# Attention and two MoE layers on one Trainium2 core: two jobs change between VectorE and ScalarE, and two query tiles share one PSUM evacuation

## The chip, the cores and the metric

The kernel runs on one core of a Trainium2 chip. The metric is device time in microseconds from the start of the program to its end; three runs of the kernel before gave 1155.38, 1155.15 and 1152.6 us, median 1155.15 us. All engine names are those of the profile: PE is TensorE, DVE is VectorE, ACT is ScalarE, POOL is GpSimd, SP is the queue that issues the DMAs.

## The reference

Thresholded softmax attention over 4 sequences of 576 tokens with 8 heads of 64, then two feed-forward layers over the 2304 tokens (512 to 2048 to 512 columns each):

```python
scores = scale * np.matmul(q, k.transpose(0, 1, 3, 2))
thresh = np.max(scores, axis=-1, keepdims=True) - tau
scores = np.where(scores >= thresh, scores, -1000000000.0)
attn = softmax(scores)                     # over the last axis
x = (attn @ v), heads side by side         # (2304, 512)
h = x @ moe_w_in;  x = (h * np.clip(h + 3.0, 0.0, 6.0) / 6.0) @ moe_w_out
h = x @ moe2_w_in; out = (np.maximum(h, 0.0) ** 2) @ moe2_w_out
```

The weights arrive as 64-bit floats. The kernel needs them as 32-bit floats and then as two parts of reduced precision (a high and a low part) for TensorE.

## The kernel before, in words

The work falls into attention (4 sequences, 4 pairs of heads each, 9 query tiles of 128 rows per pair: 144 score tiles) and eight feed-forward blocks (layer 1 and layer 2 for each sequence). The attention of sequence 0 runs first and alone; the attention of sequence b+1 is interleaved with the two feed-forward blocks of sequence b. In the last 250 us only feed-forward is left.

**One score tile.** PE multiplies q by k into a PSUM tile `s` (L244 for sequence 0, L248 later). DVE reduces it to the row minimum `nm` (L254; the scores are negated, so this is the maximum). The threshold `thr` is `nm` plus the constant `tau_a` (L255: on POOL for sequence 0, on DVE for the three later sequences). ACT makes the exponential `e` with `nm` as bias (L261). DVE multiplies it by the comparison with `thr` and sums the row (L268), which is the last read of `s`. ACT and POOL split `e` into two 16-bit parts `p` (L274 to L276), and a DMA transposes them into `pt` (L278).

**The product with v.** `av` (L296) runs five tiles later: 14 matmuls into a PSUM tile `o` from the pool `ps_a` of two buffers. That pool also holds the transposes of q, k and the outputs (`tps`, `xT`) and a small maximum (`vm`, which DVE reads at L202 and works up in L204 to L206). ACT scales each `o` by the reciprocal of the row sum into the SBUF tile `os` (L304, 64 columns per query tile; L301 for the shared tail tile). `finish` transposes `os` for the feed-forward layers.

**The PSUM pool of the matmuls.** `s`, the hidden products `hp` (L525) and the outputs `y` (L559) share the pool `ps_s` of three buffers. A buffer is free again when DVE has read it for the last time: L268 for `s`, L530 or L536 for `hp`, L565 for `y` (ACT, L563, for the first quarter of a block).

**The weights.** 64 chunks of 128 x 512 are loaded as pairs of 32-bit words (`wd`), numbered 0 to 63 in the order of use. `w_convert` makes 32-bit floats of them: ACT scales the high words into `wc` (L462), DVE shifts `wc` left by 3 (L464) and merges the top three bits of the low words into it (L465, result `wraw`), and SP stores the chunk to DRAM for later reuse (L468). Then ACT and POOL split it into `wh` and `wl` (L484, L485). All 64 conversions are over by 393 us; from then on chunks are reloaded from DRAM, and DVE makes `wl`.

A scheduler sets the order on each engine by its own timing model. Once built, every engine runs its instructions strictly in that order.

Of the kernel before, what the change touches and what calls it, by code (L numbers as in the profile page):

```python
# [10 lines left out]
F32 = mybir.dt.float32  # L11
# [3 lines left out]
I32 = mybir.dt.int32  # L15
U16 = mybir.dt.uint16
AF = mybir.ActivationFunctionType
# [5 lines left out]
LAG = 5  # L23
LOADS = (2, 4, 6)
FIRST_W = 14
N_G, N_WC, N_PT = 3, 3, 5
NWD, NRAW = 3, 4
N_S, N_ACC = 3, 2
# [3 lines left out]
def attention_moe_moe_kernel(  # L32
# [191 lines left out]
    def make_jobs(u):  # L224
        js = []
        order = [(0, 0), (0, 1), (0, 2), (0, 3), ("t", 4), (1, 0), (1, 1), (1, 2), (1, 3)]
        for hd, t in order:
            j = Job()
            j.u, j.hd, j.t = u, hd, t
            js.append(j)  # L230
        return js
# [19 lines left out]
    def soft1(j):  # L251
        j.nm = st.tile([P, 1], F32, name="nm")
        j.thr = st.tile([P, 1], F32, name="thr")
        nc.vector.tensor_reduce(out=j.nm, in_=j.s, axis=AX.XY, op=ALU.min)  # L254
        (nc.gpsimd if j.u.b == 0 else nc.vector).tensor_tensor(out=j.thr, in0=j.nm, in1=tau_a, op=ALU.add)  # L255
        if j.u.b == 0:

            j.e = me.tile([P, S], F32R, name="gh", bufs=NQ + 1).bitcast(F32).rearrange("p (a b) -> p a b", a=2)
        else:
            j.e = at.tile([P, 2, HALF], F32, name="e", bufs=2)  # L260
        nc.scalar.activation(out=j.e, in_=j.s, func=AF.Exp, bias=j.nm, scale=-1.0)  # L261
# [21 lines left out]
        nc.gpsimd.tensor_scalar(out=r, in0=r, scalar1=1e-9, scalar2=u.vsc, op0=ALU.add, op1=ALU.mult)  # L283
        nc.vector.reciprocal(out=r, in_=r)

    def av(j):

        u = j.u
        o = ps_a.tile([P, 512], F32, tag="acc", name="o")
        hs = slice(0, 2) if j.hd == "t" else slice(j.hd, j.hd + 1)  # L290
        w = 2 * D if j.hd == "t" else D
        ops = [(i, P, u.v1, i if i <= NT else i - NT - 1) for i in range(2 * NT + 1)]
        ops += [(i, TAIL if i == NT else P, u.v2, i) for i in range(NT + 1)]
        ops.sort(key=lambda x: x[0])
        for i, (c, m, vv, vc) in enumerate(ops):
            nc.tensor.matmul(o[:, 0:w], lhsT=j.pt[0:m, c, :], rhs=vv[0:m, hs, vc, :], start=i == 0, stop=i == len(ops) - 1)  # L296
        if j.n == 0:
            u.os = at.tile([P, NT + 1, P], F32, name="os", bufs=2)
        if j.hd == "t":
            for h in range(2):  # L300
                nc.scalar.activation(out=u.os[own[h], NT, 0:D], in_=o[own[h], h * D:h * D + D], func=AF.Copy, scale=u.sm[own[h], 2 * NT:2 * NT + 1])  # L301
        else:
            c = j.hd * NT + j.t
            nc.scalar.activation(out=u.os[:, j.t, j.hd * D:j.hd * D + D], in_=o[:, 0:D], func=AF.Copy, scale=u.sm[:, c:c + 1])  # L304

    def finish(u, half):

# [21 lines left out]
    def attention():  # L329

        us = []
        for b, p in units:
            u = Unit()
            u.b, u.p = b, p
            us.append(u)
        all_jobs = []
        for i, u in enumerate(us):
            u.i = i
            js = make_jobs(u)
            for n, j in enumerate(js):  # L340
                j.first = n == 0
                j.n = n
                j.last = n == len(js) - 1
            all_jobs += js
        load_qk(us[0], "k")
        setup()
        load_qk(us[0], "q")
        load_v(us[0])
        for _ in prep_steps(us[0]):
            pass  # L350
        load_qk(us[1], "k")
        load_qk(us[1], "q")
        load_v(us[1])
        n = len(all_jobs) // B
        pr = yield from run(us, all_jobs[0:n], None)
        yield from run(us, all_jobs[n:], pr)

    def run(us, all_jobs, pr):
        n = len(all_jobs)
        for i in range(n + LAG):  # L360
# [9 lines left out]
            if i >= 1 and i - 1 < n:  # L370
# [3 lines left out]
                    recips(jj.u, 2 * NT, 1)  # L374
                elif jj.t % 2:
                    recips(jj.u, jj.hd * NT + jj.t - 1, 2)
            done = [i - LAG] if all_jobs[0].u.b == 0 else [i - LAG - 1, i - LAG] if (i - LAG) % 2 else []
            done = [all_jobs[x] for x in done if 0 <= x < n]
            for j in done:
                av(j)  # L380
            for j in done:
                if j.hd == 1 and j.t % 2:
                    finish(j.u, j.t // 2)
            if i < n and pr is not None:
# [68 lines left out]
    def w_convert(i):  # L453


        src, kind, f = wseq[i]
        d = w_raw[i]
        hi = d[:, :, 1]
        c = wt.tile([P, 512], F32, name="wc", bufs=N_WC)
        t = wt.tile([P, 512], F32, name="wraw", bufs=NRAW)  # L460

        nc.scalar.activation(out=c, in_=hi.bitcast(F32), func=AF.Prelu, scale=2.0 ** -112, alpha=2.0 ** 32)  # L462
        ci = c.bitcast(I32)
        nc.vector.tensor_scalar(out=ci, in0=ci, scalar1=3, scalar2=None, op0=ALU.logical_shift_left)  # L464
        nc.vector.scalar_tensor_tensor(out=t.bitcast(I32), in0=d[:, :, 0], scalar=29, in1=ci, op0=ALU.logical_shift_right, op1=ALU.bitwise_or)  # L465
        key = (id(src), kind, f)
        dr = scr.tile([P, 512], F32, name=f"scr{i}")
        nc.sync.dma_start(out=dr, in_=t)  # L468
        wscr[key] = dr
        w_raw[i] = t  # L470
# [205 lines left out]
```

## Time and profile before

| | |
|---|---|
| median of three runs | 1155.15 us |
| the profiled execution's own time | 1153.59 us |
| its span, first to last instruction | 1151.8 us |
| PE busy | 1097.4 us (95%) |
| DVE, ACT, POOL busy | 766.3, 717.2, 592.1 us |
| mean granted TensorE clock over the span | 0.983 |

Busy time is the union of an engine's instructions. The granted clock is a share of full speed: 1.00 is 2.4 GHz and 0.50 is 1.2 GHz, and a value between is a stretch with some of both. The profiled execution's own time is 1.79 us more than its span.

### The profile page before, as it was taken

The numbers are of one execution on the slowest core, as the hardware profiler recorded it, in microseconds if no ns is written. First come the engines' busy times: TensorE is split into PE (matmuls) and PEld (weight loads), VectorE is DVE, ScalarE is ACT, GpSimd is POOL, SyncE is SP. The second block draws the span as 40 slices with busy tenths as digits, with TensorE's granted clock in tenths as the row PEclk, the third lists the DMA queues.
The fourth block names the chain that finished last, engine by engine and source line by source line (L and its number), as shares of the span: only waits on it lengthen the run. The fifth ranks groups of instructions, "written<-read, shape, count | busy, mean of one in ns | idle before, by whom it ended". The sixth has DMA issues, their size and how long they took to land.

```text
span 1151.8 us, 24221 instructions
## 1 busy us (share of the span) xinstructions
PE 1097.4 (95%) x9136; PEld 1041.9 (90%) x9136; DVE 766.3 (67%) x1393; ACT 717.2 (62%) x1345; POOL 592.1 (51%) x654
## 2 busy tenths in 40 slices
PE   6788899988999999999999999999999999999998
PEld 4566798888988999999999999999999999999998
DVE  6887799988788765767766756766756443445342
ACT  7886677767767766656765666666665455434442
POOL 5975577778677654444534355353643242224111
PEclk9998899999999999999999999999999999999999
DMA  8999899889798454566464544544444333223221
GB/s 199 204 177 196 221 249 263 227 242 249 186 263 218 129 141 114 121 135 137 112 141 118 136 124 112 125 116 100 115 120 111 85 107 91 84 83 90 76 65 42
DMA packets 286660, 167.66 MB, mean 146 GB/s; under 512 B 219216, under 2 KB 247888, under 8 KB 286544
## 3 DMA queue, kind: packets, MB, share of 16 engines
q1 hardware_dynamic: 286544, 166.12, 57.7%
q8 instruction: 72, 1.18, 0.4%
q14 instruction: 44, 0.36, 0.1%
HBM read 98.57 MB, written 21.50 MB: 104 GB/s over the span
## 4 chain that ended last, share of the span: by engine, by line
PE 68%; DVE 2%; DMA 2%; issue 1%; ACT 1%; POOL 1%; SPq 0%; DVEq 0%; ACTq 0%
PE y L559 29%; PE hp L525 29%; PE o L296 4%; PE s L248 4%; DMA vraw<-in_v_dram 1%; PE tps L141 1%; DVE wraw L465 1%; PE ot L586 1%; DVE e L268 1%; DMA wd<-in_moe_w_in_dram 0%; PE xT L310 0%; DMA wd<-in_moe_w_out_dram 0%; DVE wc L464 0%; DVE ya L565 0%; DVE nm L254 0%
## 5 line engine op out<-in xcount | busy, mean ns | idle before, releaser
L539 POOL TENSOR_TENSOR gl<-g,gh 128x576 fp32r<-128x576 f32 x128 | 193.2, 1511 | 265.9 <-ACT gh L538 265.1
L559 PE MATMUL y<-gh,who 128*128 128x288 f32 x1024 | 227.4, 303 | 7.1 <-DVE g L530 3.0
L525 PE MATMUL hp<-xh,whi 128*128 128x288 f32 x1024 | 226.4, 303 | 7.8 <-DVE e L268 6.5
L559 PE MATMUL y<-gh,wlo 128*128 128x288 f32 x1024 | 222.3, 298 | 0.0
L525 PE MATMUL hp<-xh,wli 128*128 128x288 f32 x1024 | 221.8, 298 | 0.0
L525 PE MATMUL hp<-xl,whi 128*128 128x288 f32 x1024 | 221.4, 298 | 0.0
L559 PE MATMUL y<-gl,who 128*128 128x288 f32 x1024 | 218.6, 298 | 0.0
L525 PEld LDWEIGHTS hp<-xh,whi 128*128 128x128 f32 x1024 | 164.7, 190 | 10.2 <-issue 3.9
L559 PEld LDWEIGHTS y<-gh,who 128*128 128x128 f32 x1024 | 165.4, 190 | 9.0 <-issue 6.0
L525 PEld LDWEIGHTS hp<-xh,wli 128*128 128x128 f32 x1024 | 166.3, 190 | 0.2
L559 PEld LDWEIGHTS y<-gh,wlo 128*128 128x128 f32 x1024 | 166.2, 190 | 0.1
L525 PEld LDWEIGHTS hp<-xl,whi 128*128 128x128 f32 x1024 | 165.8, 190 | 0.3
L559 PEld LDWEIGHTS y<-gl,who 128*128 128x128 f32 x1024 | 164.5, 190 | 0.0
L296 PE MATMUL o<-v,pt 128*128 128x64 f16 (+1 forms) x2016 | 124.6, 200 | 17.1 <-DMA pt<-gl 8.5
L254 DVE TENSOR_REDUCE nm<-s 128x1 f32<-128x576 f32 x144 | 108.2, 751 | 48.7 <-PE s L248 38.7
L296 PEld LDWEIGHTS <-pt 128*128 128x128 f16 x2016 | 91.9, 99 | 47.8 <-DMA pt<-gl 13.5
L276 POOL TENSOR_TENSOR p<-e,p 128x512 f16<-128x512 f32 x108 | 129.7, 1201 | 0.0
L565 DVE TENSOR_TENSOR ya<-y,ya 128x576 f32<-128x576 f32 (+1 forms) x97 | 71.9, 749 | 79.9 <-PE y L559 79.0
L484 ACT ACTIVATE who<-wraw 128x512 fp32r<-128x512 f32 x128 | 79.6, 628 | 61.9 <-PE y L559 39.4
L268 DVE SCALAR_TENSOR_TENSOR e<-s,thr,e 128x576 f32<-128x576 f32 x108 | 87.9, 814 | 33.0 <-ACT e L261 30.6
L485 DVE TENSOR_TENSOR wlo<-wraw,who 128x512 fp32r<-128x512 f32 x96 | 79.1, 833 | 45.3 <-ACT who L484 42.7
L261 ACT ACTIVATE e<-s,nm 128x576 f32<-128x576 f32 x108 | 79.7, 738 | 34.3 <-DVE nm L254 29.9
(89 smaller groups left out, 1727.0 us busy)
## 6 DMA issues: line engine op xcount, KB each, us to landing
wraw<-scr SPq DMA_DIRECT2D x192, 256.0 KB, 2.7
wd<-in_moe_w_in_dram SPq DMA_DIRECT2D x32, 512.0 KB, 5.3
scr<-wraw SPq DMA_DIRECT2D x64, 256.0 KB, 3.5
wd<-in_moe_w_out_dram SPq DMA_DIRECT2D x32, 512.0 KB, 4.7
kraw<-in_k_dram SPq DMA_DIRECT2D x16, 256.0 KB, 3.4
qraw<-in_q_dram SPq DMA_DIRECT2D x16, 256.0 KB, 3.5
vraw<-in_v_dram SPq DMA_DIRECT2D x16, 256.0 KB, 3.3
out_dram<-wd SPq DMA_DIRECT2D x16, 256.0 KB, 2.9
```

The costliest lines, as they stand in the source:

```text
L248: nc.tensor.matmul(s[:, half, 0:HALF], lhsT=u.qs[sl][:, cs], rhs=u.ks[sl][:, kk, c], start=i == 0, stop=i == len(ops) - 1)
L254: nc.vector.tensor_reduce(out=j.nm, in_=j.s, axis=AX.XY, op=ALU.min)
L261: nc.scalar.activation(out=j.e, in_=j.s, func=AF.Exp, bias=j.nm, scale=-1.0)
L268: nc.vector.scalar_tensor_tensor(out=j.e, in0=j.s, scalar=j.thr, in1=j.e, op0=ALU.is_le, op1=ALU.mult, accum_out=u.sm[:, col:col + 1])
L276: nc.gpsimd.tensor_tensor(out=p16[:, S + TAIL:], in0=e[:, 0:NT * P], in1=p16[:, 0:NT * P], op=ALU.subtract)
L296: nc.tensor.matmul(o[:, 0:w], lhsT=j.pt[0:m, c, :], rhs=vv[0:m, hs, vc, :], start=i == 0, stop=i == len(ops) - 1)
L484: nc.scalar.activation(out=h, in_=t, func=AF.Copy)
L485: (nc.gpsimd if fresh else nc.vector).tensor_tensor(out=l, in0=t, in1=h.bitcast(F32), op=ALU.subtract)
L525: nc.tensor.matmul(hp[:, a, 0:HALF], lhsT=w[:, cs], rhs=x[c][:, a * HALF:(a + 1) * HALF], start=i == 0, stop=i == 3 * NC - 1)
L539: nc.gpsimd.tensor_tensor(out=gl, in0=gf, in1=gh.bitcast(F32), op=ALU.subtract)
L559: nc.tensor.matmul(a[:, k_, 0:HALF], lhsT=w_hl[wuse[(tag, "o", f)]][w][:, cs], rhs=g[f][:, k_ * HALF:(k_ + 1) * HALF], start=i == 0, stop= ...
L565: nc.vector.tensor_tensor(out=y, in0=av_, in1=y, op=ALU.add)
```

## The change

Three things are edited. From chunk 10 on, every second chunk (10, 12, ..., 62: 27 of 64) gets the top bits of its low words from ACT, as a scaled and rounded 16-bit number written over the low words; DVE then does shift and merge in one instruction. The 108 thresholds of sequences 1 to 3 are made by ACT. And for these sequences two query tiles of a head share one PSUM tile `o`, with 28 matmuls one after the other, and one DVE product with the two reciprocals as a broadcast operand writes both into `os`: 48 products in place of 96 ACT instructions. Sequence 0 and the tail tiles keep theirs.

```diff
@@ -23,6 +23,7 @@
 LAG = 5
 LOADS = (2, 4, 6)
 FIRST_W = 14
+FIRST_DVE = 10
 N_G, N_WC, N_PT = 3, 3, 5
 NWD, NRAW = 3, 4
 N_S, N_ACC = 3, 2
@@ -252,7 +253,10 @@
         j.nm = st.tile([P, 1], F32, name="nm")
         j.thr = st.tile([P, 1], F32, name="thr")
         nc.vector.tensor_reduce(out=j.nm, in_=j.s, axis=AX.XY, op=ALU.min)
-        (nc.gpsimd if j.u.b == 0 else nc.vector).tensor_tensor(out=j.thr, in0=j.nm, in1=tau_a, op=ALU.add)
+        if j.u.b == 0:
+            nc.gpsimd.tensor_tensor(out=j.thr, in0=j.nm, in1=tau_a, op=ALU.add)
+        else:
+            nc.scalar.activation(out=j.thr, in_=j.nm, func=AF.Identity, bias=tau_a)
         if j.u.b == 0:
 
             j.e = me.tile([P, S], F32R, name="gh", bufs=NQ + 1).bitcast(F32).rearrange("p (a b) -> p a b", a=2)
@@ -283,25 +287,31 @@
         nc.gpsimd.tensor_scalar(out=r, in0=r, scalar1=1e-9, scalar2=u.vsc, op0=ALU.add, op1=ALU.mult)
         nc.vector.reciprocal(out=r, in_=r)
 
-    def av(j):
-
-        u = j.u
+    def av(js):
+
+        u, j = js[0].u, js[0]
         o = ps_a.tile([P, 512], F32, tag="acc", name="o")
+        if u.os is None:
+            u.os = at.tile([P, NT + 1, P], F32, name="os", bufs=2)
         hs = slice(0, 2) if j.hd == "t" else slice(j.hd, j.hd + 1)
         w = 2 * D if j.hd == "t" else D
         ops = [(i, P, u.v1, i if i <= NT else i - NT - 1) for i in range(2 * NT + 1)]
         ops += [(i, TAIL if i == NT else P, u.v2, i) for i in range(NT + 1)]
         ops.sort(key=lambda x: x[0])
-        for i, (c, m, vv, vc) in enumerate(ops):
-            nc.tensor.matmul(o[:, 0:w], lhsT=j.pt[0:m, c, :], rhs=vv[0:m, hs, vc, :], start=i == 0, stop=i == len(ops) - 1)
-        if j.n == 0:
-            u.os = at.tile([P, NT + 1, P], F32, name="os", bufs=2)
+        for n, j in enumerate(js):
+            for i, (c, m, vv, vc) in enumerate(ops):
+                nc.tensor.matmul(o[:, n * w:n * w + w], lhsT=j.pt[0:m, c, :], rhs=vv[0:m, hs, vc, :], start=i == 0, stop=i == len(ops) - 1)
+        j = js[0]
         if j.hd == "t":
             for h in range(2):
                 nc.scalar.activation(out=u.os[own[h], NT, 0:D], in_=o[own[h], h * D:h * D + D], func=AF.Copy, scale=u.sm[own[h], 2 * NT:2 * NT + 1])
-        else:
+        elif len(js) == 1:
             c = j.hd * NT + j.t
             nc.scalar.activation(out=u.os[:, j.t, j.hd * D:j.hd * D + D], in_=o[:, 0:D], func=AF.Copy, scale=u.sm[:, c:c + 1])
+        else:
+            c = j.hd * NT + j.t
+            r = u.sm[:, c:c + 2].rearrange("p (t o) -> p t o", o=1).to_broadcast([P, 2, D])
+            nc.vector.tensor_tensor(out=u.os[:, j.t:j.t + 2, j.hd * D:j.hd * D + D], in0=o[:, 0:2 * D].rearrange("p (t d) -> p t d", t=2), in1=r, op=ALU.mult)
 
     def finish(u, half):
 
@@ -336,6 +346,7 @@
         all_jobs = []
         for i, u in enumerate(us):
             u.i = i
+            u.os = None
             js = make_jobs(u)
             for n, j in enumerate(js):
                 j.first = n == 0
@@ -374,11 +385,13 @@
                     recips(jj.u, 2 * NT, 1)
                 elif jj.t % 2:
                     recips(jj.u, jj.hd * NT + jj.t - 1, 2)
-            done = [i - LAG] if all_jobs[0].u.b == 0 else [i - LAG - 1, i - LAG] if (i - LAG) % 2 else []
-            done = [all_jobs[x] for x in done if 0 <= x < n]
-            for j in done:
-                av(j)
-            for j in done:
+            x = i - LAG
+            if 0 <= x < n:
+                j = all_jobs[x]
+                if j.hd == "t" or j.u.b == 0:
+                    av([j])
+                elif j.t % 2:
+                    av([all_jobs[x - 1], j])
                 if j.hd == 1 and j.t % 2:
                     finish(j.u, j.t // 2)
             if i < n and pr is not None:
@@ -461,8 +474,14 @@
 
         nc.scalar.activation(out=c, in_=hi.bitcast(F32), func=AF.Prelu, scale=2.0 ** -112, alpha=2.0 ** 32)
         ci = c.bitcast(I32)
-        nc.vector.tensor_scalar(out=ci, in0=ci, scalar1=3, scalar2=None, op0=ALU.logical_shift_left)
-        nc.vector.scalar_tensor_tensor(out=t.bitcast(I32), in0=d[:, :, 0], scalar=29, in1=ci, op0=ALU.logical_shift_right, op1=ALU.bitwise_or)
+        if i < FIRST_DVE or i % 2:
+            nc.vector.tensor_scalar(out=ci, in0=ci, scalar1=3, scalar2=None, op0=ALU.logical_shift_left)
+            nc.vector.scalar_tensor_tensor(out=t.bitcast(I32), in0=d[:, :, 0], scalar=29, in1=ci, op0=ALU.logical_shift_right, op1=ALU.bitwise_or)
+        else:
+
+            d16 = d.rearrange("p f t -> p (f t)").bitcast(U16).rearrange("p (f t) -> p f t", t=4)
+            nc.scalar.activation(out=d[:, :, 0], in_=d16[:, :, 1], func=AF.Copy, scale=2.0 ** -13, bias=-4095.5 / 8192)
+            nc.vector.scalar_tensor_tensor(out=t.bitcast(I32), in0=ci, scalar=3, in1=d[:, :, 0], op0=ALU.logical_shift_left, op1=ALU.bitwise_or)
         key = (id(src), kind, f)
         dr = scr.tile([P, 512], F32, name=f"scr{i}")
         nc.sync.dma_start(out=dr, in_=t)
```

The scheduler sets the order anew. PE has the same order up to the matmul of `vm` that starts at 137.7 us in the profile. Two places show what changes.

DVE, around the reduction `vsc<-vm` of one head pair of sequence 1 (the place at 285 us of the profile; L464 and L465 are shift and merge, L255 the threshold). Before:

```order
L464 TENSOR_SCALAR wc<-wc 128x512
L254 TENSOR_REDUCE nm<-s 128x1
L255 TENSOR_TENSOR thr<-nm,tau_a 128x1
L536 TENSOR_TENSOR g<-g,hp 128x576
L465 SCALAR_TENSOR_TENSOR wraw<-wd,wc 128x512
L464 TENSOR_SCALAR wc<-wc 128x512
L202 TENSOR_REDUCE vsc<-vm 128x1
L465 SCALAR_TENSOR_TENSOR wraw<-wd,wc 128x512
L204 TENSOR_SCALAR vsc<-vsc 128x1
L268 SCALAR_TENSOR_TENSOR e,sm<-s,thr,e 128x576
```

After (L478 and L479 are shift and merge, L484 the merge that shifts, L314 the product of two query tiles, L203 to L207 the work on `vsc`):

```order
L272 SCALAR_TENSOR_TENSOR e,sm<-s,thr,e 128x576
L478 TENSOR_SCALAR wc<-wc 128x512
L484 SCALAR_TENSOR_TENSOR wraw<-wc,wd 128x512
L288 RECIPROCAL sm<-sm 128x1
L203 TENSOR_REDUCE vsc<-vm 128x1
L205 TENSOR_SCALAR vsc<-vsc 128x1
L206 RECIPROCAL vsc<-vsc 128x1
L207 TENSOR_SCALAR vsc<-vsc 128x1
L255 TENSOR_REDUCE nm<-s 128x1
L314 TENSOR_TENSOR os<-o,sm 128x2x64
L555 TENSOR_TENSOR g<-g,hp 128x576
```

The threshold and one of two shifts are gone from this place, a product has come, and the four instructions on `vsc` stand next to each other.

ACT, around the second chunk that the change touches (`p_2101` and `p_2184` are the same two tiles in both; L462 is the scaling of the high words, L304 the evacuation of one query tile). Before:

```order
L274 ACTIVATE p_2101<-e 128x576
L212 ACTIVATE v_2195<-vraw,vsc 128x640
L304 ACTIVATE os<-o,sm 128x64
L261 ACTIVATE e<-s,nm 128x576
L462 ACTIVATE wc<-wd 128x512
L187 ACTIVATE q_st_93<-tps,qs 64x256
L484 ACTIVATE whi<-wraw 128x512
L563 ACTIVATE ya<-y 128x576 x2
L274 ACTIVATE p_2184<-e 128x576
L304 ACTIVATE os<-o,sm 128x64
```

After (L475 is the scaling of the high words, L483 the new instruction on the low words, L259 the threshold):

```order
L278 ACTIVATE p_2101<-e 128x576
L475 ACTIVATE wc<-wd 128x512
L483 ACTIVATE wd<-wd 128x512
L503 ACTIVATE whi<-wraw 128x512
L188 ACTIVATE q_st_93<-tps,qs 64x256
L259 ACTIVATE thr<-nm,tau_a 128x1
L265 ACTIVATE e<-s,nm 128x576
L582 ACTIVATE ya<-y 128x576
L475 ACTIVATE wc<-wd 128x512
L582 ACTIVATE ya<-y 128x576
L188 ACTIVATE q_st_93<-tps,qs 64x64
L278 ACTIVATE p_2184<-e 128x576
```

Each exponential now has its threshold directly ahead of it, the touched chunk has two instructions in a row, and the evacuations L304 are gone from ACT.

## Rows read from the trace of the kernel before

**Rows 1.** Windows, us: engines' busy time (count), PE's granted clock, DMA share, GB/s

```profile
0.00:106.00 106.00, 83.80 (x701) 61.11 (x702) 81.78 (x198) 84.30 (x178) 76.53 (x152) 0.95 0.88 191
106.00:144.00 38.00, 31.10 (x217) 27.67 (x217) 25.99 (x46) 22.94 (x45) 21.94 (x21) 0.82 0.91 222
144.00:400.00 256.00, 237.50 (x1985) 225.22 (x1984) 220.60 (x377) 182.40 (x348) 189.34 (x180) 0.97 0.86 227
400.00:900.00 500.00, 498.01 (x4321) 481.94 (x4320) 336.03 (x636) 322.79 (x603) 238.28 (x259) 1.00 0.51 121
900.00:1152.00 252.00, 247.00 (x1922) 245.97 (x1920) 101.88 (x140) 104.76 (x174) 66.00 (x45) 1.00 0.27 80
```

**Rows 2.** PE's waits from 144 to 400 us: total us, times, longest

```profile
PE hp L525 <- DVE e L268: 5.3, 5, 1.3
PE o L296 <- DVE vsc L202: 3.1, 3, 1.7
PE y L559 <- DVE g L530: 2.7, 1, 2.7
...
PE hp L525 <- ACT g L532: 0.5, 1, 0.5
...
PE hp L525 <- DVE ya L565: 0.3, 1, 0.3
```

**Rows 3.** DVE from 144 to 400 us by line: busy us, mean ns, idle before

```profile
L465 DVE SCALAR_TENSOR_TENSOR wraw<-wd,wc 128x512 int32<-128x512 int32 x53 | 56.0, 1056 | 5.6 <-POOL wlo L485 1.9 <-DMA scr<-wraw 1.4 <-POOL wli L485 1.1
L464 DVE TENSOR_SCALAR wc<-wc 128x512 int32<-128x512 int32 x53 | 42.8, 807 | 11.1 <-ACT wc L462 10.6
...
L255 DVE TENSOR_TENSOR thr<-nm,tau_a 128x1 f32<-128x1 f32 x36 | 18.8, 522 | 0.4
```

**Rows 4.** Three DVE lines over the whole run: duration ns min/median/max

```profile
L255 DVE TENSOR_TENSOR thr<-nm,tau_a x108: 141/159/1426, 106.4 to 893.5; 128x1 f32<-128x1 f32 x108
L464 DVE TENSOR_SCALAR wc<-wc x64: 405/608/1659, 21.1 to 371.3; 128x512 int32<-128x512 int32 x64
L268 DVE SCALAR_TENSOR_TENSOR e<-s,thr,e x108: 797/817/820, 109.7 to 893.7; 128x576 f32<-128x576 f32 x108
```

**Rows 5.** DVE lines over the whole run, for the new product

```profile
L202 DVE TENSOR_REDUCE vsc<-vm 128x1 f32<-128x128 f32 x16 | 4.6, 285 | 5.9 <-PE vm L200 5.8
L318 DVE TENSOR_TENSOR xl<-xT,xh 128x256 fp32r<-128x256 f32 x8 | 3.4, 420 | 4.6 <-ACT xh L317 4.5
```

**Rows 6.** ACT from 144 to 400 us by line

```profile
L462 ACT ACTIVATE wc<-wd 128x512 f32<-128x512 f32 x53 | 35.3, 667 | 14.4 <-DMA wd<-in_moe_w_in_dram 7.8 <-DMA wd<-in_moe_w_out_dram 6.4
L261 ACT ACTIVATE e<-s,nm 128x576 f32<-128x576 f32 x36 | 26.6, 738 | 13.6 <-DVE nm L254 12.9 <-POOL wli L485 0.2
L304 ACT ACTIVATE os<-o,sm 128x64 f32<-128x64 f32 x29 | 8.8, 309 | 6.5 <-PE o L296 6.4
```

**Rows 7.** ACT lines over the whole run, for the threshold

```profile
L301 ACT ACTIVATE os<-o,sm 64x64 f32<-64x64 f32 x32 | 9.8, 307 | 3.8 <-PE o L296 3.5
L320 ACT ACTIVATE xr<-xT 64x64 f32<-64x64 f32 x24 | 5.1, 212 | 0.1
```

**Rows 8.** DVE in order of time before 285 us: start us, us

```profile
278.52 1.29 DVE L464 TENSOR_SCALAR wc<-wc 128x512 int32<-128x512 int32 x1 [0.20 <-ACT wc L462]
...
280.64 0.44 DVE L255 TENSOR_TENSOR thr<-nm,tau_a 128x1 f32<-128x1 f32 x1
...
283.36 1.62 DVE L464 TENSOR_SCALAR wc<-wc 128x512 int32<-128x512 int32 x1
284.90 0.28 DVE L202 TENSOR_REDUCE vsc<-vm 128x1 f32<-128x128 f32 x1
```

**Rows 9.** PE in order of time after it, and the window that follows

```profile
285.23 1.50 PE L296 MATMUL o<-v,pt 128*128 128x64 f16 x28 [1.71 <-DVE vsc L202]
287.64 0.85 PE L525 MATMUL hp<-xh,whi 128*128 128x288 f32 x2 [0.92 <-DVE e L268]
...
288.00:292.00 4.00, 4.00 (x18) 4.00 (x18) 3.91 (x7) 3.12 (x6) 2.81 (x3) 0.50 0.55 164
```

**Rows 10.** DVE and PE in order of time around the longest wait

```profile
247.09 1.91 DVE L465 SCALAR_TENSOR_TENSOR wraw<-wd,wc 128x512 int32<-128x512 int32 x1
...
249.25 0.41 DVE L464 TENSOR_SCALAR wc<-wc 128x512 int32<-128x512 int32 x1
...
252.03 0.72 PE L559 MATMUL y<-gh,who 128*128 128x288 f32 x2 [2.68 <-DVE g L530]
```

**Rows 11.** Windows, the first and second part of the conversions

```profile
144.00:240.00 96.00, 90.93 (x761) 86.64 (x760) 87.24 (x153) 68.91 (x129) 70.55 (x70) 0.98 0.95 249
240.00:400.00 160.00, 146.57 (x1229) 138.58 (x1226) 133.37 (x225) 113.49 (x220) 118.79 (x111) 0.97 0.80 213
```

More of the change, by code (lines that the diff above doesn't have):

```diff
@@ L301, in av @@
                 nc.scalar.activation(out=u.os[own[h], NT, 0:D], in_=o[own[h], h * D:h * D + D], func=AF.Copy, scale=u.sm[own[h], 2 * NT:2 * NT + 1])
+        elif len(js) == 1:
+            c = j.hd * NT + j.t
+            nc.scalar.activation(out=u.os[:, j.t, j.hd * D:j.hd * D + D], in_=o[:, 0:D], func=AF.Copy, scale=u.sm[:, c:c + 1])
         else:
             c = j.hd * NT + j.t
-            nc.scalar.activation(out=u.os[:, j.t, j.hd * D:j.hd * D + D], in_=o[:, 0:D], func=AF.Copy, scale=u.sm[:, c:c + 1])
+            r = u.sm[:, c:c + 2].rearrange("p (t o) -> p t o", o=1).to_broadcast([P, 2, D])
+            nc.vector.tensor_tensor(out=u.os[:, j.t:j.t + 2, j.hd * D:j.hd * D + D], in0=o[:, 0:2 * D].rearrange("p (t d) -> p t d", t=2), in1=r, op=ALU.mult)
     def finish(u, half):
```

## The prediction

> **What bounds the kernel now.** I read the windows first, since one busy share for the whole run mixes three different stages. From 400 us to the end PE has 745.0 of 752 us busy at full clock, of the missing 7 us 5 lie after 900 us [rows 1]. Nothing that other engines do there can give time back, as long as they don't fall behind. Before 106 us the change touches nothing that counts: sequence 0 keeps its threshold on POOL and its evacuations on ACT, and chunks 0 to 9 are converted as before. So the change is won or lost between 106 and 400 us. From 106 to 144 us PE idles 6.9 us at a clock of 0.82, but only four thresholds and chunk 10 are affected there; I count nothing for it. From 144 to 400 us PE is busy 237.5 of 256 us, which leaves 18.5 us idle, and the granted clock of 0.97 is worth another 0.03 x 256 = 7.7 us. That is a pool of 26.2 us [rows 1].
>
> Next, who ends PE's waits in that stretch. Ten of the eleven kinds of wait name DVE, with 20 waits and 18.0 us together; ACT ends one of 0.5 us [rows 2]. PE waits for a PSUM buffer that DVE has yet to read. DVE is busy 220.6 of 256 us (86%), ACT 182.4 (71%) [rows 1]. DVE is the engine that PE waits for, and the conversion of the weights fills it: shift and merge take 42.8 and 56.0 us there, the thresholds another 18.8 us [rows 3].
>
> **What leaves and enters DVE, 144 to 400 us.** The 53 shifts of the stretch are chunks 11 to 63, so 26 of them are touched: 26 x 0.807 = 21.0 us [rows 3]. The 36 thresholds of 0.522 us are 18.8 us [rows 3]. The 29 evacuations that leave ACT [rows 6] come back as about 15 products on DVE. Such a product, 128 elements from PSUM, is not in the trace. Below it lies the reduction of 128 elements from PSUM with 0.285 us, above it the subtraction of 256 elements from PSUM with 0.420 us [rows 5]; the element count speaks for the first, and I take 0.29, 4.4 us in all. The sum is 21.0 + 18.8 - 4.4 = 35.4 us off DVE, which takes it from 220.6 to 185.2 us, from 86% to 72%.
>
> This is the upper end. A threshold lasts 141 ns at best, 159 in the middle and 1426 at worst, a shift 405 to 1659, while the long L268, which reads one operand from PSUM, stays within 797 to 820 [rows 4]. A good part of the two first is thus waiting, and the next instruction of the same kind may take that waiting over. With the shortest durations and the dearest product the relief is 26 x 0.405 + 36 x 0.141 - 15 x 0.420 = 9.3 us. The Trainium skill explains the stretching (SBUF: State Buffer, "SBUF: two separate sides"): a VectorE instruction with two SBUF inputs, or in a two-port mode, and a GpSimd instruction exclude each other for the whole of the instruction. The trace agrees with it in the 159 and 1426 ns, and by that rule the new product, with one operand in PSUM, would not be stretched.
>
> **What enters and leaves ACT there.** The new instruction on the low words has the element count of L462, which reads the high words at the same stride, with 0.667 us [rows 6]: 26 x 0.667 = 17.3 us. That it reads 16-bit words and writes at a stride is not in the trace; the price could be higher, and a rival below uses it. A threshold on ACT has one element and a bias operand. An instruction of 64 columns takes 0.212 us without and 0.307 us with an operand per partition [rows 7]; I take 0.25, so 36 x 0.25 = 9.0 us. By the Trainium skill (ScalarE: Activation LUTs, "What ACT_TABLE_LOAD costs") an activation with such an operand costs about 0.28 us plus its columns; that would make it 10.1 us. The 29 evacuations of 0.309 us that go are 9.0 us [rows 6]. ACT gains 17.3 us, from 182.4 to 199.7 us, 78%. So the two engines change places, but the busier one then stands at 78% and not at 86%.
>
> **What PE gets from it.** I looked at what stood ahead of DVE's late instruction in two waits. At 285.23 us PE had waited 1.71 us for the reduction of `vsc`. DVE had last idled just before 278.52; since then it ran two shifts of 1.29 and 1.62 us and a threshold of 0.44 [rows 8]. One shift and the threshold go, about 1.9 us, and the new order puts the reduction earlier still. This wait goes, and with it the 0.92 us behind it and the four microseconds at half clock that follow [rows 9]. The longest wait, 2.68 us before 252.03, is another matter: a merge of 1.91 us and other work that stays are ahead of it, and only short shifts of the kind of the 0.41 us at 249.25 can go [rows 10]. It mostly stays. I take it that 55% of the 18.0 us goes, 10 us; this share is an estimate between these two examples. Of the 7.7 us lost to the clock about half hang on waits that go: 4 us. Against this I set 3 us for new waits on ACT: each exponential now stands behind its threshold, and each of 26 times two conversions of 0.667 us run before the next evacuation. The sum is 10 + 4 - 3 = 11 us.
>
> From 400 us on DVE has 336.0 of 500 us and ACT 322.8, and PE still idles only 2 us [rows 1]: 72 thresholds leave DVE and 32 products enter it, under the cover of a full PE. I cost that at nothing. If the cover failed, it would be in the two-buffer pool `ps_a`: `o` is now released by DVE's queue, and a late product holds up a transpose. The profiled execution's own time of 1153.59 less 11 is 1142.6. It lies 1.6 us under the median of 1155.15, from which 11 us make 1144.1. I forecast **1143.5 us**.
>
> **Rivals.**
> - *The whole pool goes.* DVE at 72% might no longer hold PE at all: 1154 - 26 = 1128 us. For it speaks that DVE ends 18.0 of 18.5 us; against it the wait at 252, which has other causes. Chance 0.12.
> - *The DMAs set the pace of the conversions.* Their share is 0.95 from 144 to 240 us and 0.80 afterwards [rows 11], and ACT waited 14.2 us for chunks to land [rows 6]. Then the first part gives nothing, and only 240 to 400 us does: 13.4 us idle and 4.8 us of clock, of which a third is 6 us, and some of it comes back as a wait for the next chunk. 1149 us, 2 to 6 us under now. Chance 0.15.
> - *ACT's queue takes the waits over, no change.* The thresholds sit on the way from `nm` to `e` and so of every score tile's release; 36 x 0.25 = 9 us longer there, and 26 pairs of conversions, eat what DVE returns. 1154 us. Chance 0.13.
> - *Slower: the instruction on the low words is dear.* With 182.4 + 9.0 - 9.0 + 26t, ACT reaches the 220.6 us at which DVE holds PE today when t is 1.47 us. From there PE has the same waits at ACT as it had at DVE, and the longer chain of the score tiles, up to 9 us, comes on top: 1155 + 6 = 1161 us. The same end is reached if products on DVE hold up the transposes after 400 us. Nothing in the trace has such a price, but nothing has such an access either. Chance 0.15.
> - *The change does not do what it says.* The order shows the moved instructions where the diff puts them, so I give this none.
>
> **How the numbers follow.** The forecast has 0.45, for 5 to 17 us gained (1138 to 1150). A difference within 0.3%, 3.5 us, is about what a measurement of this kernel can't tell from none. Faster: 0.45 + 0.12 + 0.10 of the DMA rival = 0.67. The same: 0.05 of that rival + 0.13 = 0.18. Slower: 0.15. For 8 times in 10 the range reaches to 1130, most of the way to the whole pool, and on the other side to 1157.5, past the rival without change; what is left out is the slower rival with most of its 0.15 and a little of the first.
>
> **What the changed profile would show.** The shifts must fall to 37, the DVE thresholds be gone, DVE stand near 72% and ACT near 78% until the last conversion. The last conversion should end some 8 to 12 us earlier than 393 us, and everything after it be shifted by as much. PE's idle time before that should be 8 to 11 us, and its waits should name DVE less and ACT more often. The product should last about 0.29 us without stretching, the instruction on the low words under 0.75 us. I am wrong if that one takes over 1.4 us, if PE's waits before 400 us keep their 18 us under other names, or if idle time of more than 3 us appears on PE after the last conversion.

## The result and the profile after

The changed kernel takes 1136.38 us (median of five runs, 1134.32 to 1139.84), the kernel before beside it 1155.15. The ratio is 0.9844, with a 95% interval from 0.9821 to 0.9867: 18 us faster. The forecast was 1143.5 us; the time lies in its range, at 1.6 times the gain. The profiled execution took 1134.32 us with a span of 1132.5 us, 19.3 under the span before. It is the fastest of the five and has their highest granted clock, 0.990 where the five have a median of 0.988.

First the windows of the changed kernel, with the columns of [rows 1] (us, then busy time and count of PE, weight load, DVE, ACT, POOL, then clock, DMA share, GB/s):

```profile
0.00:106.00 106.00, 84.00 (x698) 61.72 (x698) 84.61 (x198) 84.28 (x178) 77.82 (x154) 0.95 0.92 194
106.00:144.00 38.00, 31.79 (x247) 28.93 (x244) 25.46 (x49) 28.28 (x58) 25.43 (x24) 0.87 0.95 235
144.00:400.00 256.00, 244.90 (x2096) 233.60 (x2095) 196.34 (x341) 202.47 (x390) 194.78 (x185) 1.00 0.88 231
400.00:900.00 500.00, 499.68 (x4348) 483.85 (x4347) 316.85 (x590) 316.88 (x599) 228.79 (x250) 1.00 0.52 121
```

From 144 to 400 us PE now idles 11.1 us in place of 18.5, at a clock of 1.00 in place of 0.97. But a fixed window holds more of the program than it did (2096 matmuls where there were 1985), since the program is further along by then: the last merge began at 392.9 us and begins now at 376.0. For loads I therefore compare the stretch from 144 us to the last conversion, here in the kernel before:

```profile
144.00:393.60 249.60, 231.09 (x1930) 219.30 (x1929) 214.83 (x367) 176.94 (x338) 185.39 (x175) 0.97 0.86 228
```

and in the changed one, with what is left up to 900 us:

```profile
144.00:376.70 232.70, 221.92 (x1907) 211.42 (x1906) 182.13 (x313) 185.91 (x360) 177.37 (x170) 1.00 0.92 241
376.70:900.00 523.30, 522.66 (x4536) 506.04 (x4535) 331.06 (x618) 333.44 (x630) 246.20 (x265) 1.00 0.52 121
```

DVE falls from 86% to 78%, ACT rises from 71% to 80%. For the time the clean account is PE's over the whole run, since both kernels issue the same 9136 matmuls. These are the lines of busy time of the pages before and after (busy us, share of the span, instructions):

```profile
PE 1097.4 (95%) x9136; PEld 1041.9 (90%) x9136; DVE 766.3 (67%) x1393; ACT 717.2 (62%) x1345; POOL 592.1 (51%) x654
PE 1088.1 (96%) x9136; PEld 1035.0 (91%) x9136; DVE 718.8 (63%) x1306; ACT 730.4 (64%) x1384; POOL 590.0 (52%) x654
```

PE's busy time falls from 1097.4 to 1088.1 us: 9.3 us for the same matmuls, most of it from the higher mean clock, 0.990 for 0.983 (0.007 x 1152 = 8.1 us). Its idle time falls from 54.4 to 44.4 us, 10.0 us. Together they are the 19.3 us of the span. This split is that of one execution each, and the clock differs between executions of one kernel: the kernel before ran 60 times beside the experiments below, in 1147.4 to 1158.3 us, with clocks from 0.980 to 0.989 and a median of 0.984. By the medians the clock rose by 0.004, which is 4.6 us of 1150, and the rest of the 18 us would be idle time (an estimate from these clocks). By place, the idle time from 144 us to the last conversion went from 18.5 to 10.8 us, that from 106 to 144 us from 6.9 to 6.2; after the last conversion and up to 900 us it was 2.0 and is 0.6.

PE's waits from 144 to 400 us after the change (total us, times, longest; the five longest of ten rows), to be held against [rows 2]:

```profile
PE y L578 <- DVE e L272: 3.2, 5, 1.2
PE hp L544 <- DVE e L272: 3.2, 2, 1.9
PE s L249 <- DVE g L549: 1.5, 1, 1.5
PE tps L142 <- ACT xr L330: 0.9, 1, 0.9
PE hp L544 <- DVE g L549: 0.7, 1, 0.7
```

The wait for `vsc` (3.1 us) is gone and so is the one of 2.68 us. What is left still names DVE, and ACT, with 1.2 us in two waits for 0.5 in one, hardly more than before. At the place of the wait at 285 us, DVE now runs with gaps under 0.1 us from the shift into the reduction:

```profile
266.48 0.95 DVE L478 TENSOR_SCALAR wc<-wc 128x512 int32<-128x512 int32 x1 [0.26 <-ACT wc L475]
267.35 0.68 DVE L484 SCALAR_TENSOR_TENSOR wraw<-wc,wd 128x512 int32<-128x512 int32 x1
268.12 0.16 DVE L288 RECIPROCAL sm<-sm 128x1 f32<-128x1 f32 x1
268.19 0.27 DVE L203 TENSOR_REDUCE vsc<-vm 128x1 f32<-128x128 f32 x1
```

Of the two shifts and the threshold of [rows 8] one shift of 0.95 us is left there; PE starts its `o` at 268.89 us with no wait in front of it, and the granted clock, which stood at 0.50 after that place [rows 9], is 1.00 in every stretch of 4 us from 236 to 300 us.

The prices of the new instructions, over the whole run (duration ns min/median/max, then first to last start):

```profile
L314 DVE TENSOR_TENSOR os<-o,sm x48: 272/283/293, 137.5 to 905.8; 128x128 f32<-128x128 f32 x48
L259 ACT ACTIVATE thr<-nm,tau_a x108: 275/294/312, 107.6 to 872.8; 128x1 f32<-128x1 f32 x108
L483 ACT ACTIVATE wd<-wd x27: 650/669/700, 130.7 to 351.9; 128x512 int32<-128x512 uint16 x27
L484 DVE SCALAR_TENSOR_TENSOR wraw<-wc,wd x27: 664/779/1966, 133.6 to 372.3; 128x512 int32<-128x512 int32 x27
L478 DVE TENSOR_SCALAR wc<-wc x37: 408/730/1593, 20.7 to 356.0; 128x512 int32<-128x512 int32 x37
```

### The profile page after: what moved, and what is told of

The parts are those of the page before. It is cut to its first block, busy times and chain, and to the rows that moved or that the text cites. A ratio compares the mean times of both kernels' runs of the same rounds, so it can differ in the third digit from the quotient of the medians.

```text
span 1132.5 us, 24055 instructions
## 1 busy us (share of the span) xinstructions
PE 1088.1 (96%) x9136; PEld 1035.0 (91%) x9136; DVE 718.8 (63%) x1306; ACT 730.4 (64%) x1384; POOL 590.0 (52%) x654
## 4 chain that ended last, share of the span: by engine, by line
PE 71%; ACT 3%; DVE 2%; DMA 1%; issue 1%; POOL 1%; SPq 0%; DVEq 0%; ACTq 0%; POOLq 0%
PE y L578 30%; PE hp L544 29%; PE o L303 5%; PE s L249 4%; DMA wd<-in_moe_w_out_dram 1%; PE tps L142 1%; PE ot L605 1%; DMA wd<-in_moe_w_in_dram 1%; DVE wraw L484 0%; ACT e L265 0%; PE xT L320 0%; DVE wraw L479 0%; ACT wc L475 0%; ACT wd L483 0%; DVE ya L584 0%
## 5 line engine op out<-in xcount | busy, mean ns | idle before, releaser
L544 PE MATMUL hp<-xh,wli 128*128 128x288 f32 x1024 | 219.0, 295 | 0.0
L544 PE MATMUL hp<-xl,whi 128*128 128x288 f32 x1024 | 218.8, 296 | 0.0
L255 DVE TENSOR_REDUCE nm<-s 128x1 f32<-128x576 f32 x144 | 107.9, 750 | 51.6 <-PE s L249 46.7
L280 POOL TENSOR_TENSOR p<-e,p 128x512 f16<-128x512 f32 x108 | 132.0, 1222 | 0.0
L557 ACT ACTIVATE gh<-g 128x576 fp32r<-128x576 f32 x128 | 86.8, 680 | 13.6 <-DVE g L555 8.0
```

Source lines behind the costliest of these rows:

```text
L280: nc.gpsimd.tensor_tensor(out=p16[:, S + TAIL:], in0=e[:, 0:NT * P], in1=p16[:, 0:NT * P], op=ALU.subtract)
L544: nc.tensor.matmul(hp[:, a, 0:HALF], lhsT=w[:, cs], rhs=x[c][:, a * HALF:(a + 1) * HALF], start=i == 0, stop=i == 3 * NC - 1)
L557: nc.scalar.activation(out=gh, in_=gf, func=AF.Copy)
```

## The experiments

Each ran 5 to 12 times beside the kernel before; ratios are to it, with 95% intervals. Windows, rows and the ends of the conversions are those of one execution of each kernel. My theory was that DVE's load before the last conversion sets the end, so that each edit is worth what it takes off DVE. The rivals: that pairing the outputs gains by itself, and that ACT's load counts as well. To turn ratios into microseconds I multiply their distance from 1 by 1155; the intervals are 1.4 to 3.3 us to either side. One thing holds for all of them: the scheduler sets the order anew for every kernel. Even with the changed kernel as the base, as in d_shift and a_twice, PE's order differs from the change's from 147 or 148 us on. So the price of an edit includes that of its order, and no run separates the two.

| kernel | what of the change it has | ratio | last conversion ends, us |
|---|---|---|---|
| e1_conv | conversion | 0.9932 [0.9908, 0.9955] | 385.2 |
| e2_thr | thresholds | 0.9974 [0.9959, 0.9988] | 396.9 |
| e3_pair | pairs | 0.9930 [0.9909, 0.9950] | 385.9 |
| e4_conv_thr | conversion, thresholds | 0.9917 [0.9892, 0.9943] | 389.1 |
| e5_conv_pair | conversion, pairs | 0.9893 [0.9865, 0.9922] | 382.6 |
| the change | all three | 0.9844 [0.9821, 0.9867] | 376.7 |

**The conversion alone** (e1_conv): the kernel before with this edit only.

```diff
-        nc.vector.tensor_scalar(out=ci, ...shift left 3)
-        nc.vector.scalar_tensor_tensor(... in0=d[:, :, 0], scalar=29, in1=ci, ...)
+        if i < FIRST_DVE or i % 2:
...
+            nc.scalar.activation(out=d[:, :, 0], in_=d16[:, :, 1], func=AF.Copy, ...)
+            nc.vector.scalar_tensor_tensor(... in0=ci, scalar=3, in1=d[:, :, 0], ...)
```

> The kernel before with the split conversion alone (low words of chunks 10, 12, ..., 62 on ACT). Theory (DVE's load until the last conversion sets the time): 26 shifts of 0.81 us leave DVE there, about half of the 35 us that the whole change takes off it, so about half of the 18.8 us: 8 to 11 us faster, the last conversion near 384 us, granted clock 144 to 380 us at 0.98 or above. Rival (the new order of the products with v gives the gain): 0 to 3 us faster.

It gained 7.9 us, just under the theory's 8 to 11. Its window up to the last conversion:

```profile
144.00:385.20 241.20, 225.62 (x1934) 215.43 (x1934) 191.06 (x340) 191.47 (x364) 183.06 (x175) 0.99 0.89 235
```

DVE has 23.8 us less than before and ACT 14.5 more.

**The thresholds alone** (e2_thr).

```diff
-        (nc.gpsimd if j.u.b == 0 else nc.vector).tensor_tensor(out=j.thr, in0=j.nm, in1=tau_a, op=ALU.add)
+        if j.u.b == 0:
+            nc.gpsimd.tensor_tensor(out=j.thr, in0=j.nm, in1=tau_a, op=ALU.add)
+        else:
+            nc.scalar.activation(out=j.thr, in_=j.nm, func=AF.Identity, bias=tau_a)
```

> The kernel before with the thresholds of sequences 1 to 3 on ACT alone. Theory: 18.8 us leave DVE, most of it waiting for GpSimd; the merges may take over some of that waiting: 5 to 9 us faster. Rival (waiting is only handed on, and a threshold costs its 0.14 us): 36 x 0.14 = 5 us of DVE work, 1 to 2 us faster. Second rival (the longer chain through ACT costs): slower by up to 9 us.

3.0 us, the smallest of the three and between the ranges of the theory and its first rival, although 18.8 us of DVE time leave by the rows [rows 3]. The window shows only half of that gone (214.83 to 205.50). Much of the other half is in the merges: their mean rises from 1056 ns [rows 3] to 1184, 6.7 us over 52 of them. First the window, then their row:

```profile
144.00:396.90 252.90, 234.32 (x1987) 222.52 (x1984) 205.50 (x328) 184.81 (x373) 183.77 (x174) 0.99 0.87 224
L468 DVE SCALAR_TENSOR_TENSOR wraw<-wd,wc 128x512 int32<-128x512 int32 x52 | 61.3, 1184 | 3.7 <-POOL wli L488 1.6 <-issue 0.8
```

In the profiled executions the last conversion ends even 3.3 us later than before, while the whole is 1.4 us faster. The end of the conversions is a marker of the stage, not the time itself.

**The pairs alone** (e3_pair).

```diff
-        for i, (c, m, vv, vc) in enumerate(ops):
-            nc.tensor.matmul(o[:, 0:w], ...)
+        for n, j in enumerate(js):
+            for i, (c, m, vv, vc) in enumerate(ops):
+                nc.tensor.matmul(o[:, n * w:n * w + w], ...)
...
-            nc.scalar.activation(out=u.os[:, j.t, ...], in_=o[:, 0:D], func=AF.Copy, scale=...)
+            nc.vector.tensor_tensor(out=u.os[:, j.t:j.t + 2, ...], in0=o[...], in1=r, op=ALU.mult)
```

> The kernel before with two query tiles per product alone. Theory: it puts 15 x 0.284 = 4 us on DVE before 400 us and takes 9 us off ACT, which PE does not wait for: between no change and 3 us slower. Rival (the gain is in the order and in the PSUM buffers that the pairing frees): 5 us faster or more.

8.1 us, as much as the conversion, with DVE no less loaded than before (213.63 us in a shorter stretch, 88%):

```profile
144.00:385.90 241.90, 226.09 (x1920) 214.86 (x1919) 213.63 (x380) 169.86 (x306) 186.53 (x174) 0.99 0.89 234
```

This contradicts my theory, which had no change to 3 us slower: an edit that puts work on the fullest engine and takes it off one at 71% gains 8 us.

**Conversion and thresholds** (e4_conv_thr): the change without the `av` part.

```diff
-            x = i - LAG
...
-                    av([all_jobs[x - 1], j])
+            done = [i - LAG] if all_jobs[0].u.b == 0 else [i - LAG - 1, i - LAG] if (i - LAG) % 2 else []
```

> The change without the pairing: split conversion and thresholds on ACT, products with v as before. Theory: DVE has 4 us less than in the whole change, ACT 9 us more: 16 to 20 us faster than before, within 3 us of the whole change. Rival (pairing gives the gain): at most 12 us faster. Rival (ACT is now the engine that PE waits for, so 9 us more on it count): 10 to 14 us faster, with PE's waits naming ACT for 5 us or more.

9.6 us, where the theory had 16 to 20. It has the lowest DVE load of the six (179.79 of 245.1 us, 73%) and the highest ACT load (197.93 us, 81%), and falls 8.4 us short of the whole change, which has 2 us more on DVE and 12 less on ACT:

```profile
144.00:389.10 245.10, 229.33 (x1938) 218.44 (x1937) 179.79 (x305) 197.93 (x397) 177.61 (x172) 0.99 0.89 230
```

PE's waits name ACT there for only 0.3 us.

**What in the pairs gains.** Two kernels take them apart. p1_pair_act keeps the shared PSUM tile but empties it with two ACT instructions; p2_group keeps only the new grouping, each tile with its own `o`. The rest is as before.

```diff
-            nc.vector.tensor_tensor(out=u.os[:, j.t:j.t + 2, ...], in0=o[...], in1=r, op=ALU.mult)
+            for n in range(2):
+                nc.scalar.activation(out=u.os[:, j.t + n, ...], in_=o[:, n * D:n * D + D], func=AF.Copy, scale=u.sm[:, c + n:c + n + 1])
```

> The kernel before with two query tiles in one PSUM tile, but evacuated by two ACT instructions as before. Pairing alone gave 8 us with no relief of DVE. Theory B (the shared PSUM tile and the unbroken 28 matmuls and transposes give it): 5 to 9 us faster. Rival C (it is the 9 us that leave ACT): no change to 2 us faster.

```diff
-                    av([all_jobs[x - 1], j])
+                    av([all_jobs[x - 1]])
+                    av([j])
```

> The kernel before with its products with v called in the new pairs (tiles 0 and 1, 2 and 3 of a head, the tail tile alone), but a PSUM tile and an ACT evacuation for each. Theory B (shared PSUM tile): no change, within 2 us. Rival D (it is the new grouping, which lets a whole half be finished at one place): 5 to 9 us faster.

p1_pair_act: 0.9975 [0.9957, 0.9993], 2.9 us, between theory B and rival C. p2_group: 1.0006 [0.9993, 1.0018], nothing. So the grouping is worth nothing, the shared tile about 3 us (barely clear of none), and moving the evacuations from ACT to DVE the other 5 (the two intervals, of e3_pair and p1_pair_act, don't meet). p1_pair_act has 7.3 us more on ACT than e3_pair and 2.9 us less on DVE, though in a longer stretch, for its profiled execution was the slowest of its twelve (1154.99 us, median 1150.7):

```profile
144.00:396.30 252.30, 229.48 (x1928) 217.55 (x1927) 210.77 (x367) 177.20 (x338) 183.92 (x175) 0.99 0.87 226
```

Why the shared tile gains was not taken further; it halves the number of tiles that `ps_a` hands out for `o`, but no run changes that alone.

**The load of each engine by itself.** d_shift gives DVE back its 27 shifts, into a tile that nobody reads; a_twice gives ACT one more instruction of 128 x 512 for each of the 27 chunks, a copy of the high words, also unread. Everything else is the changed kernel.

```diff
+            z = wt.tile([P, 512], I32, name="wz", bufs=2)
+            nc.vector.tensor_scalar(out=z, in0=ci, scalar1=3, scalar2=None, op0=ALU.logical_shift_left)
```

> The whole change with 27 shifts of 128 x 512 put back on DVE for the same chunks, written to a tile that nobody reads (work added, nothing left out). Theory A (DVE's load until the last conversion counts): loses 6 to 9 us of the 18.8, 10 to 13 us faster than before. Rival (the gain is that the merge no longer waits for a shift; load is covered): within 3 us of the whole change, 16 to 20 us faster.

```diff
+            z = wt.tile([P, 512], F32, name="wz", bufs=2)
+            nc.scalar.activation(out=z, in_=d[:, :, 1].bitcast(F32), func=AF.Copy)
```

> The whole change with a second ACT instruction of 128 x 512 for each of the 27 chunks, written to a tile that nobody reads: the price of 1.34 us that the slower rival of the prediction is about. Prediction's step (ACT reaches DVE's old 86% at 1.47 us and holds PE as DVE did): ACT near 84% until the last conversion, the gain mostly lost, 0 to 8 us faster than before. Rival (ACT has slack that PE doesn't see, since its instructions do not wait for GpSimd): 13 to 18 us faster than before.

d_shift: 0.9909 [0.9891, 0.9926], so 7.5 us of the 18 lost, as its theory A had it. Its extra shifts take 18.3 us by their own row (the busy time and mean ns, then the idle time before them):

```profile
L485 DVE TENSOR_SCALAR wz<-wc 128x512 int32<-128x512 int32 x26 | 18.3, 702 | 7.0 <-ACT wc L475 6.8
```

and DVE's busy time up to the last conversion rises by 15.4 us, to 197.56:

```profile
144.00:385.60 241.60, 227.94 (x1917) 217.18 (x1916) 197.56 (x340) 187.50 (x362) 178.59 (x171) 0.98 0.89 232
```

a_twice: 0.9931 [0.9915, 0.9948], 10.0 us lost, so 8 us faster than before, the upper end of what the prediction's step gave. This is its extra instruction, and its window:

```profile
L484 ACT ACTIVATE wz<-wd 128x512 f32<-128x512 f32 x26 | 17.2, 663 | 0.0
144.00:388.70 244.70, 230.17 (x1939) 219.58 (x1938) 181.84 (x319) 203.18 (x394) 181.81 (x175) 0.97 0.89 231
```

So a microsecond added to either engine of the changed kernel costs about half of one. Both extra instructions also stand between the scaling of a chunk and its merge and make each conversion's way longer; the runs do not take this apart from the load. That ACT's counts as much could not be read from PE's waits. In a_twice they still name other engines (144 us to the last conversion):

```profile
PE y L580 <- POOL gl L560: 4.4, 2, 2.9
PE hp L546 <- DVE e L272: 2.9, 5, 1.6
PE y L580 <- DVE e L272: 2.9, 2, 2.4
PE y L580 <- DVE ya L586: 2.1, 2, 1.7
PE y L580 <- ACT gh L559: 1.4, 2, 1.1
```

How it can count is seen one link further back. These are waits of ACT in e3_pair, of DVE in the changed kernel, and of ACT in the changed kernel, each from 144 us to the last conversion:

```profile
ACT e L262 <- DVE nm L255: 19.3, 18, 2.8
```

```profile
DVE e L272 <- ACT e L265: 9.3, 12, 1.9
DVE nm L255 <- PE s L249: 7.3, 5, 3.5
```

```profile
ACT thr L259 <- DVE nm L255: 10.3, 9, 1.9
ACT p L278 <- DVE e L272: 5.4, 6, 1.6
```

A score tile goes from DVE (`nm`) to ACT (`e`) and back to DVE (the product, its last reader). PE waits for the last reader, and the row has DVE's name; how late it runs depends on both engines' queues. That this is the whole of ACT's price was not tested.

**Further along the same way.** v1_all takes the new conversion for every chunk from 10 on, v4_pair0 also pairs the outputs of sequence 0, v3_thr_pool puts the thresholds of all sequences on POOL, and e5_conv_pair puts those of sequences 1 to 3 back on DVE. All start from the changed kernel.

```diff
-        if i < FIRST_DVE or i % 2:
+        if i < FIRST_DVE:
```

> The whole change with every chunk from 10 on split, not every second. DVE loses another 27 shifts before the last conversion (some 20 us), ACT gains 27 x 0.67 = 18 us and stands near 88%. Theory (a microsecond on either engine there costs about half a microsecond): within 4 us of the whole change, 15 to 22 us faster than before. Rival (DVE alone counts): 26 us faster or more. Rival (ACT is now the bound): 8 to 13 us faster.

```diff
-                if j.hd == "t" or j.u.b == 0:
+                if j.hd == "t":
```

> The whole change with the tiles of sequence 0 paired too: 32 ACT evacuations become 16 products on DVE in the first 106 us, where ACT is busy 80% and DVE 77%. Theory (pairing relieves ACT and the PSUM pool wherever both engines are busy): 1 to 4 us faster than the whole change. Rival (in this stretch PE waits for the transposing DMAs, and a pair waits for the later of two): no change or up to 4 us slower than the whole change.

```diff
-        if j.u.b == 0:
-            nc.gpsimd.tensor_tensor(out=j.thr, in0=j.nm, in1=tau_a, op=ALU.add)
-        else:
-            nc.scalar.activation(out=j.thr, in_=j.nm, func=AF.Identity, bias=tau_a)
+        nc.gpsimd.tensor_tensor(out=j.thr, in0=j.nm, in1=tau_a, op=ALU.add)
```

> The whole change with the thresholds of sequences 1 to 3 on GpSimd, as those of sequence 0 are, and not on ACT. ACT loses 36 x 0.29 = 10 us before the last conversion, GpSimd gains 36 x 0.22 = 8 us. Theory (ACT's microseconds count by about half): 2 to 5 us faster than the whole change, 20 to 24 us faster than before. Rival (a threshold queues behind GpSimd's 1.2 to 1.7 us instructions and holds up the last read of the score tile): 2 us slower than the whole change or more.

```diff
+        (nc.gpsimd if j.u.b == 0 else nc.vector).tensor_tensor(out=j.thr, in0=j.nm, in1=tau_a, op=ALU.add)
```

> The change without its thresholds, which stay on DVE: split conversion and pairing. Alone these gave 7.8 and 8.1 us. Theory (the gains add up; a threshold moved is worth the 2 to 3 us that it gave alone): 14 to 17 us faster than before. Rival (both take away the same waits): 8 to 12 us faster, and the thresholds are worth 7 us or more in this company.

None beats the change. v1_all: 0.9882 [0.9861, 0.9903], so 13.6 us faster than before and 4.4 behind the change, with intervals that just overlap. That lies under the theory's 15 to 22 us and just over the 8 to 13 of the rival with ACT as the bound. Its window:

```profile
144.00:382.10 238.10, 226.05 (x1908) 215.72 (x1907) 158.55 (x288) 200.82 (x388) 172.48 (x170) 0.98 0.90 236
```

DVE is down to 67% and ACT up to 84%; DVE lost 23.6 us more than in the change, at 14.9 more on ACT, and nothing is gained by it. The rows do not show why. Of the 5.3 us between the spans of the two profiled executions PE's idle time makes 1.3 (45.7 for 44.4) and its busy time 4.0 (1092.1 for 1088.1), at a clock of 0.985 for 0.990, and the clock differs by as much between executions of one kernel. PE's waits there still name DVE first:

```profile
PE hp L544 <- DVE e L272: 5.2, 5, 2.0
PE y L578 <- DVE e L272: 3.7, 2, 2.8
```

With DVE at 67% and 23.6 us lighter, less load on DVE no longer helps. Here the name in the wait alone would mislead.

v4_pair0: 0.9872 [0.9850, 0.9894], no better, as its rival had it. Before 106 us ACT gets lighter (79.06 for 84.28 us), and PE waits somewhat longer for the transposes that a pair needs both of:

```profile
PE o L303 <- DMA pt<-gl: 7.7, 5, 2.7
```

(6.1 us in seven waits in the changed kernel.) More of its idle time comes from 106 to 144 us, 8.6 us for 6.2. v3_thr_pool: 0.9892 [0.9870, 0.9914], 5.5 us behind the change, as its rival had it. On POOL a threshold lasts 286 ns on average from 106 to 400 us (over the whole run 180 at best, 772 at worst), and DVE now waits for it:

```profile
DVE e L269 <- POOL thr L256: 3.9, 4, 1.3
```

e5_conv_pair, the change without moved thresholds, gains 12.4 us, between its two expectations, and is 5.7 us behind the change. So the thresholds are worth 3.0 us alone and 5.7 in company; their intervals overlap. The three edits alone sum to 19.0 us, the change has 18.0. Thresholds with pairs and without the conversion was not run.

**One line through the runs.** For the change, e1 to e4, p1, p2, d_shift and a_twice I fitted the gain to the busy times from 144 us to the last conversion: 0.63 us for each of DVE's, 0.55 for each of ACT's, and 2.7 us for the shared tile, with no miss above 2.8 us. For the other four it gives 12.5 us (v3, measured 12.5), 9.9 (e5, 12.4), 18.8 (v4, 14.8) and 24.9 (v1, 13.6). The busy times themselves depend on how long the stretch became, so this line describes the runs and proves no cause. It is 4 us off in v4_pair0, which also changes the stretch before 106 us, and breaks in v1_all, which has less on DVE than any of the nine.

## Why the prediction was right, and where its sizes were off

- *Place.* Right. The gain lies before the last conversion; after 400 us PE idles no more than before. The 106 to 144 us that I counted at nothing gave 0.7 us of idle time, and the clock rose there from 0.82 to 0.87, 0.05 x 38 = 1.9 us.
- *Idle time.* The forecast was 10 us less, 3 given back to ACT, so 7 in all; from 144 us to the last conversion it fell by 7.7 in the profiled executions, and by 10.0 over the whole run. The wait at 285 us went, as said. The longest one, which I thought would mostly stay, went too.
- *Clock.* The forecast was "about half" of 7.7 us, 4 us. In the profiled execution all of it came back from 144 us to the last conversion (0.97 to 1.00): before, the clock stood at half there from 214.6, 252.1 and 286.3 us, the last two behind the waits of [rows 10] and [rows 9], and none of the three is left. The last alone was half of this time, which is the half that I had counted. But that execution has the highest clock of the five. By the medians, 0.988 for 0.984, the clock gives 4.6 us, near the forecast. So the runs do not settle how much of the missing gain is clock.
- *Off DVE.* 35.4 us forecast, 32.7 measured by the windows (214.83 to 182.13). That the shifts and thresholds are partly waiting that others take over was right: thresholds alone took off 9.3, not 18.8 us. DVE ended at 78% and not 72%, since the stretch became shorter with it.
- *Onto ACT.* 17.3 us forecast, 9.0 measured: the worst-sized term. By rows the parts are close: 25 x 0.670 = 16.7, 34 x 0.292 = 9.9, less the evacuations of 8.8 [rows 6], make 17.8 us. But some 4 us of other ACT work no longer fall before the last conversion. And ACT's instructions overlap their neighbours: up to the last conversion their durations sum to 197.9 us where the busy time, a union, is 176.9, and to 211.6 where it is 185.9 after. So nearly 5 us more are overlap. The forecast added durations to a union. The low words cost 0.669 us against 0.667, so the dear instruction of the slower rival did not come. a_twice pays 0.670 + 0.663 = 1.33 us per chunk, near the 1.47 us at which I had the sign turn, and is still 8 us faster than before, with ACT at 83%. By its loss of 0.58 us for each microsecond, 1.47 us would cost 2 more, an estimate, and still leave 6. The rival's threshold was therefore too low: it had ACT alone at 86% as bad as DVE at 86%, with nothing for DVE's relief.
- *Thresholds on ACT.* I took 0.25 us; 0.294 is the median. The Trainium skill (ScalarE: Activation LUTs, "What ACT_TABLE_LOAD costs") has about 0.28 us plus the columns for an activation with an operand per partition, and the trace agrees with it.
- *The product.* 0.29 us without stretching forecast, 272 to 293 ns measured, while the merges in the same stretch run from 664 to 1966. The Trainium skill (SBUF — State Buffer, "SBUF: two separate sides") has the lock for VectorE instructions with two SBUF inputs, against GpSimd instructions that read SBUF; an instruction with one operand in PSUM should escape it, and the 21 ns between shortest and longest agree.
- *Pairs.* Here the reasoning was wrong under a sum that came out near. I booked them as 4.4 us of cost on DVE, and their 9 us off ACT only against the other additions. Alone they gain 8.1 us, nearly half of the whole. The step that failed is "DVE is the engine that PE waits for": ACT's load was treated as slack below 86%, and so the pairs stood in the sum as a cost. The 8.1 us that they gain alone are about what the forecast fell short by; no run divides these seven microseconds among the terms, so that the time came out in the range owes something to luck.
- *Signs.* The shifts fell to 37, the product and the low words cost what was said, and PE's idle time from 144 us to the last conversion is 10.8 us. The last conversion ended 16.9 us earlier and not 8 to 12, and DVE's and ACT's shares, 78% and 80%, lie closer together than 72% and 78%.
- *Rivals.* That the DMAs set the pace did not hold: their share rose from 0.86 to 0.92 as the conversions ran faster. That ACT takes the waits over is half true: by the fitted line its load costs 0.55 us a microsecond, and the change gains because it takes 33 us off one engine and puts 9 on the other. The whole pool did not go: 10.8 us of idle time are left.

## What to carry to other kernels

The engine that ends the waits is only the last link. Where a tile passes two engines in turn, count both loads: here a move was worth about half a microsecond for each that left the one, less as much for each that entered the other, and a short PSUM-reading instruction on DVE was a cheap place for work. If a trace shows half-clock stretches behind waits, count the clock with the waits that go, and compare the clocks of several executions before a part of the gain is put down to it. Do not carry the move far past the point where the two are equally full: here one more step, every chunk instead of every second, gained nothing and seems to have lost 4 us.

## What the runs showed of the hardware

- An ACT instruction that reads 16-bit words at a stride of four and writes 32-bit integers at a stride of two lasts 650 to 700 ns for 128 x 512, no more than the 32-bit one beside it (0.670 us).
- Removing short instructions that wait long on average does not remove all of the waiting: 36 thresholds of 0.522 us left DVE and its busy time fell by 9.3 us, half of their sum, while the mean merge rose from 1056 to 1184 ns (e2_thr).
- A POOL instruction of one column lasts 180 to 772 ns, with a median of 191 (v3_thr_pool): stretched ones occur on POOL too. From 106 to 400 us they took 286 ns on average, less than the 522 ns on DVE before (144 to 400 us), and the kernel was still 5.5 us behind the change.
- The granted clock of one and the same kernel differs between executions: 0.980 to 0.989 in 60 of the kernel before, and its time from 1147.4 to 1158.3 us.
